# The order of four engines handed to a list scheduler inside the kernel, in a packed-attention plus feed-forward kernel

## The chip, the core and the metric

The kernel runs on one core of a Trainium2 chip. The core has a matrix engine (TensorE, PE in the profile, with its weight loads shown apart as PEld), a vector engine (VectorE, DVE), a scalar engine (ScalarE, ACT), a general engine (GpSimd, POOL) and a sync engine (SyncE, SP) that here only issues transfers. Each engine works through its own list of instructions in the order in which the program put them, and semaphores make one wait for another. Matmuls write to PSUM, which has 8 banks of 128 partitions by 512 fp32 numbers; ACT and DVE move the results on to SBUF. DMA queues carry data between HBM and SBUF.

The metric is the device time of one execution in microseconds (us).

## The reference: what is computed

For 8 batch entries and 8 heads, 32 learned "packs" `p` attend over 576 keys, and then the 576 queries attend over the 32 packed values. The result, as 4608 rows of 512, goes through a gated feed-forward layer.

```python
def _attn_ref(q, k, v, p):            # q, k, v: (8, 8, 576, 64); p: (8, 8, 32, 64)
    def sm_attn(qq, kk, vv):
        s = scale * np.matmul(qq, kk.transpose(0, 1, 3, 2))
        s = s - np.max(s, axis=-1, keepdims=True)
        a = np.exp(s)
        a = a / (np.sum(a, axis=-1, keepdims=True) + 1e-09)
        return np.matmul(a, vv)
    p_packed = sm_attn(p, k, v)
    return sm_attn(q, p_packed, p_packed)

def _moe_ref(x, w_in, w_out):         # x: (4608, 512); w_in: (512, 2048); w_out: (2048, 512)
    h = x @ w_in
    sp = np.maximum(h, 0.0) + np.log1p(np.exp(-np.abs(h)))
    g = h * erf(sp)
    return (g @ w_out).astype(np.float32)
```

`w_in` and `w_out` arrive as 64-bit floats and are turned into 32-bit ones by bit operations on the chip.

## The kernel before, in words

All 8 heads of a batch entry `b` lie side by side on the partitions. `attention(b)` (`first_attention` for `b` = 0) makes the first scores `s1` in two halves of 288 columns, their softmax `a1`, its transposes `t1` and, with `v`, the packed values `pt` (product `p`; the last 64 of the 576 keys go through a small transpose of their own, the left-over, line 368). Then it makes the second scores `s2`, again in two halves, and their softmax, which is kept as a high and a low part, `a2h` and `a2l`.

Since the second attention is linear in `pt`, the kernel multiplies `pt` into `w_in` first: `w_prime(b, j)` makes piece `j` of four of a matrix W' (tile `wp`, kept as `wph` and `wpl`). The feed-forward then runs in 128 units: one per batch entry and 128 columns `f` of the 2048. A unit's `h` is two halves (`h_part`), each of six matmuls into one of the two `ps_h` banks, evacuated by an ACT copy to `hs` (line 469). Units are gated in groups (`gate_group`, mostly of four): all Softplus, then all Erf (each needs its table of functions loaded into ACT), then on DVE a product and a split into `gh` and `gl`. Finally `o_part` adds the unit to four accumulators of 128 rows (`ps_o0` to `ps_o3`), in three matmuls each. The last 64 rows of two batch entries are collected through a DRAM buffer `rest` and done together by `o_rest` (tile `or`, 48 matmuls a pair, loaded in four tiles `g`).

PSUM is full: four banks for `o`, two for `h`, and two (`ps_m`, one tile over both) shared by scores, transposes, `p`, W' and the last `or`.

**What sets the order before.** The program text puts attention stages, weight pieces and W' pieces behind chosen units by the tables of `PLAN`. The framework's own scheduler may then move instructions on each engine; functions on ACT are held in their order (`in_turn`), conversions are held behind a named copy (`hold`), and from unit 48 on (`"strict": 48`) PE keeps exactly the text's order (`pe`). Each half of the scores and each W' piece takes the one `ps_m` tile, one at a time. Four staging buffers for 64-bit weights are borrowed from the W' pool (`EARLY`), in the order in which `do` comes to the pieces of `w_in` and `w_out`; after those, two `wst` buffers serve all weight pieces and also the `g` tiles of `or`.

Lines that the steps below touch: 87 (weight loads), 97 to 102 (their conversion), 166 to 176 (first loads), 325 and 388 (`s1`, `s2`), 350 and 399 (the two Exp), 369 (left-over copy), 374 (`p`), 391 (DVE transposes out of `s2`), 420 to 423 (W'), 443 and 446 (Softplus, Erf), 467 and 469 (`h` and its copy), 489 (`o`), 510 and 513 (`g`, `or`).

## Time and profile before

| | us |
|---|---|
| median of 3 runs (lowest, highest) | 787.98 (783.42, 790.71) |
| time of the profiled execution | 785.28 |
| its span, first to last instruction | 783.4 |
| PE busy | 732.7 (94%) |
| ACT busy | 496.8 (63%) |
| DVE busy | 436.6 (56%) |
| HBM traffic over the span | 54.00 MB read, 19.92 MB written |

The profile shows one execution. A row of a timeline gives start, length, engine, line, operation and, in brackets, how long the engine had been idle before it and who released it. Matmuls overlap: one lasts longer than the distance to the next, so their rate is read from the starts. The profile counts an fp32 matmul as two. PEclk is the clock that PE was granted, as a share of full speed.

### The profile page before, as it was taken

The page shows a single profiled execution, that of the slowest core. Times are in us where ns is not written, and L with a number is a line of the kernel's source. Part 1 is how long each engine was busy: PE and PEld are TensorE (multiplying, and loading weights), DVE is VectorE, ACT ScalarE, POOL GpSimd, SP SyncE. Part 2 cuts the span into 40 slices and gives each one's busy share as a digit, 9 for nine tenths or more (in the row PEclk, how much of TensorE's full clock was granted, in tenths as well). Part 3 has the DMA queues.
Part 4 walks back from the last instruction along what each step waited for, and adds up shares of the span by engine and source line. Part 5 has one row for each costly group of instructions (what it writes and reads, how often), then busy time and mean ns, then how long its engine had stood idle before and what let it go on. Part 6 is the DMA issues. An engine that isn't in the chain of part 4 may idle for free.

```text
span 783.4 us, 12901 instructions
## 1 busy us (share of the span) xinstructions
PE 732.7 (94%) x5008; PEld 581.9 (74%) x5008; DVE 436.6 (56%) x689; ACT 496.8 (63%) x806; POOL 8.0 (1%) x14
## 2 busy tenths in 40 slices
PE   4576899989999999999999999999999999999997
PEld 3273678668777877878777787778877887788885
DVE  3778967678764247544755048553674236743530
ACT  3284988788668556685767348675676457666731
POOL 0000000000101000000000000000000000000000
PEclk9986999999999999999999999999999999999999
DMA  9915153443716230223302332124212320003103
GB/s 334 337 36 192 45 170 98 163 125 99 205 33 147 60 127 13 66 68 114 96 16 65 126 90 68 24 68 153 68 43 61 118 67 13 16 14 98 41 21 121
DMA packets 66397, 74.77 MB, mean 95 GB/s; under 512 B 40224, under 2 KB 42272, under 8 KB 66336
## 3 DMA queue, kind: packets, MB, share of 16 engines
q1 hardware_dynamic: 64896, 71.27, 29.2%
q0 software_dynamic: 1152, 2.10, 1.8%
q8 instruction: 39, 0.64, 0.3%
q10 hardware_dynamic: 288, 0.59, 0.2%
q14 instruction: 22, 0.18, 0.1%
HBM read 54.00 MB, written 19.92 MB: 94 GB/s over the span
## 4 chain that ended last, share of the span: by engine, by line
PE 73%; ACT 12%; DVE 10%; DMA 3%; issue 2%; SPq 0%; DVEq 0%; ACTq 0%
PE o L489 38%; PE h L467 22%; PE or L513 5%; PE wp L420 3%; ACT t L446 2%; PE p L374 2%; ACT L446 2%; DVE hs L448 2%; ACT t L443 2%; ACT hs L469 1%; DMA g<-rest 1%; ACT L443 1%; PE s L325 1%; DVE ta L397 1%; DVE mx L396 1%
## 5 line engine op out<-in xcount | busy, mean ns | idle before, releaser
L489 PE MATMUL o<-woh,gh 128*128 128x512 f32 x512 | 201.8, 405 | 1.3 <-DVE gh L432 1.0
L489 PE MATMUL o<-woh,gl 128*128 128x512 f32 x512 | 201.8, 394 | 0.9 <-DVE gl L433 0.9
L469 ACT COPY hs<-h 128x288 f32<-128x288 f32 x256 | 98.2, 396 | 164.3 <-PE h L467 162.9
L489 PE MATMUL o<-wol,gh 128*128 128x512 f32 x512 | 200.7, 395 | 0.0
L467 PE MATMUL h<-a2h,wph 128*128 128x288 f32 x512 | 158.6, 310 | 18.0 <-ACT hs L469 10.4
L448 DVE TENSOR_TENSOR hs<-t,hs 128x576 f32<-128x576 f32 x128 | 91.8, 753 | 115.0 <-ACT t L446 115.0
L467 PE MATMUL h<-a2h,wpl 128*128 128x288 f32 x512 | 154.2, 302 | 1.0 <-DVE wpl L423 1.0
L467 PE MATMUL h<-a2l,wph 128*128 128x288 f32 x512 | 154.6, 302 | 0.0
L467 PEld LDWEIGHTS h<-a2h,wph 128*128 128x128 f32 x512 | 99.7, 195 | 47.0 <-ACT hs L469 16.2
L489 PEld LDWEIGHTS o<-woh,gh 128*128 128x128 f32 x512 | 96.6, 189 | 41.2 <-issue 23.8
L489 PEld LDWEIGHTS o<-wol,gh 128*128 128x128 f32 x512 | 96.3, 188 | 23.0 <-issue 2.1
L432 DVE CAST gh<-hs 128x576 fp32r<-128x576 f32 x128 | 58.2, 456 | 94.0 <-PE o L489 94.0
L489 PEld LDWEIGHTS o<-woh,gl 128*128 128x128 f32 x512 | 96.6, 189 | 16.6 <-issue 1.7
L467 PEld LDWEIGHTS h<-a2l,wph 128*128 128x128 f32 x512 | 99.9, 195 | 10.0 <-DVE mx L252 0.9
L467 PEld LDWEIGHTS h<-a2h,wpl 128*128 128x128 f32 x512 | 99.8, 195 | 2.4 <-DVE wpl L423 1.3
L433 DVE TENSOR_TENSOR gl<-hs,gh 128x576 fp32r<-128x576 f32 x128 | 96.2, 754 | 2.3
L443 ACT ACTIVATE t<-hs 128x576 f32<-128x576 f32 x128 | 87.4, 685 | 2.7
L446 ACT ACTIVATE t<-t 128x576 f32<-128x576 f32 x128 | 78.1, 674 | 0.4
L420 PE MATMUL wp<-w_in_sb,pt 64*32 64x512 f32 x512 | 44.3, 646 | 6.3 <-ACT a L301 3.4
L423 DVE TENSOR_TENSOR wpl<-wp,wph 128x1024 fp32r<-128x1024 f32 x32 | 39.0, 1220 | 16.7 <-ACT wph L422 16.0
L443 ACT ACT_TABLE_LOAD x37 | 47.5, 1283 | 0.7
L446 ACT ACT_TABLE_LOAD x37 | 47.5, 1283 | 0.7
(112 smaller groups left out, 565.6 us busy)
## 6 DMA issues: line engine op xcount, KB each, us to landing
q<-qT SPq DMA_DIRECT2D x32, 288.0 KB, 4.5
v<-v SPq DMA_DIRECT2D x32, 256.0 KB, 4.2
wos<-w_out SPq DMA_DIRECT2D x16, 512.0 KB, 3.7
out<-ob SPq DMA_DIRECT2D x32, 256.0 KB, 2.3
g<-rest SPq DMA_DIRECT2D x16, 512.0 KB, 3.3
k<-kT SPq DMA_DIRECT2D x26, 288.0 KB, 4.0
wi<-w_in SPq DMA_DIRECT2D x12, 512.0 KB, 4.1
rest<-gh SPq DMA_DIRECT2D x128, 32.0 KB, 1.5
```

The source lines that it names most:

```text
L374: pe(nc.tensor.matmul(po[64 * r:64 * r + 64, NK * c:NK * c + NK], values[j][0:n, 64 * (2 * c + r):64 * (2 * c + r) + 64], a1t[0:n, j, r, N ...
L420: pe(nc.tensor.matmul(ps[NK * c:NK * c + NK, r, :], pt[b][64 * r:64 * r + 64, NK * c:NK * c + NK], w_in_sb[64 * r:64 * r + 64, c, j * FB:( ...
L423: nc.vector.tensor_tensor(lo[:], ps[:], hi[:], op=ALU.subtract)
L432: nc.vector.tensor_copy(ghi[:], hs[:])
L433: nc.vector.tensor_tensor(glo[:], hs[:], ghi[:], op=ALU.subtract)
L443: in_turn(nc.scalar.activation(t[:], hs[:], AF.Softplus))
L446: in_turn(nc.scalar.activation(t[:], t[:], AF.Erf))
L448: nc.vector.tensor_tensor(hs[:], t[:], hs[:], op=ALU.mult)
L467: pe(nc.tensor.matmul(ps[:, 0:HT], w[:, r, fo:fo + P], a[:, r, c, :], start=(m == 0), stop=(m == 5)))
L469: hold.append(nc.scalar.copy(hs[:, c * HT:(c + 1) * HT], ps[:, 0:HT]).ins.name)
L489: pe(nc.tensor.matmul(acc[b][x][:], gg[:, x * P:(x + 1) * P], w[:], start=(first and n == 0), stop=(last and n == 2)))
L513: pe(nc.tensor.matmul(acc["rest"], gg, w[:], start=(k == 0 and i == 0 and n == 0), stop=(k == NFB - 1 and i == PER - 1 and n == 2)))
```

## The change

The program is first recorded and only then issued. Every instruction group becomes an `Op` with an engine, a key (the unit at which it is wanted), an estimated length and the buffers that it reads and writes. `Program.order()` plays these through: whenever an engine is free it takes the waiting `Op` with the lowest key whose buffers have room, counting 1.283 us for each change of ACT table and an extra for PE's change between tile shapes; an Exp is not taken inside a group of Softplus or Erf. The order found is then fixed on PE, ACT, DVE, SP and POOL by `line`, from the first instruction on. The tables of places in `PLAN` give way to keys.

Further edits:

- From `b` = 2 on, the second half of `s1` and of `s2` and the odd W' pieces (`j` = 1, 3) go to the two `ps_h` banks in place of `ps_m`, and are evacuated bank by bank (two smaller copies in place of one).
- The left-over of `a1`'s transposes has its own tile `a1r` (tag `rem`), and its eight matmuls of `p` are an `Op` of their own.
- The first two attentions reduce their scores straight from PSUM; the `k` of `b` = 0 is loaded in halves, and ACT's first table load stands ahead of ACT's loads.
- The four borrowed staging buffers all go to the four pieces of the second quarter of `w_in`.
- The first units' groups end after 2, 5, 8, 12, 16 units (before: 2, 5, 7, 9, 12, 14, 16).
- `or` is sixteen `Op`s of three matmuls in place of four blocks of twelve.
- The instructions on PE are the same in number and shape. ACT has 90 table loads (before 88) and 23 instructions more in all, DVE 29 more.

```diff
-    "strict": 48,
+    "lag": 5.5,
+    "steady": (0, 1, 1.5, 2, 2, 5, 5.2, 6, 7, 8, 8, 9, 10, 11),
+    "merge": (1, 1),
...
+    def order(self):
...
+            for engine, line in ready.items():
+                if free[engine] > now + 1e-9:
+                    continue
+                held, pick = set(), None
+                for i, (_, _, op) in enumerate(line):
+                    if op.run == "exp" and state["within"]:
+                        continue
...
+                    if any(room[t] < n or t in held for t, n in need.items()):
+                        held.update(need)
+                        continue
+                    pick = i
+                    break
+                if pick is None:
+                    continue
+                op = line.pop(pick)[2]
+                op.fresh = [buf for buf in op.used if buf.tag and buf not in taken]
+                for buf in op.fresh:
+                    taken.add(buf)
+                    room[buf.tag] -= 1
+                op.start, busy = now, op.busy
+                if op.run:
+                    if op.run != state["table"]:
+                        busy += self.LOAD
+                        state["table"] = op.run
+                    state["within"] = op.kind == 1
+                if engine == "PE":
+                    if op.kind != state["kind"]:
+                        busy += self.SWITCH[state["kind"]]
+                    state["kind"] = op.kind
+                free[engine] = now + busy
...
+    def line(engine, ins):
+        names = {last[x] for x in (engine, *fresh) if x in last}
+        for name in names:
+            tc.add_manual_dep(ins.ins, name, mybir.DependencyInfo(
+                mybir.DependencyClass.NoSync, mybir.DependencyReason.DATA), reason="order")
+        for x in (engine, *fresh):
+            last[x] = ins.ins.name
+        fresh.clear()
+        return ins
...
+    staged = [0]
     EARLY = ("wpl", "wpl", "wph", "wph")
...
+        tag = EARLY[staged[0]] if staged[0] < len(EARLY) else "wst"
+        staged[0] += 1
+        st = buf(tag, [P, n], name, I64)
+        dma(sent, n * P * 8, lambda: nc.sync.dma_start(st[:], src), (st,), ())
...
-    pe_last, strict = [], [False]
-
-    def pe(ins):
-
-        if strict[0] and pe_last:
-            follow(ins, pe_last[-1])
-        pe_last[:] = [ins.ins.name]
...
+    def banks_of(names, where):
+        if where == "m":
+            one = buf("ps_m", [P, 2, 512], names)
+            return [lambda: one[:, 0, :], lambda: one[:, 1, :]], (one,), lambda: one[:]
+        tags = ("ps_h", "ps_h") if where == "h" else (f"ps_o{2 * where}", f"ps_o{2 * where + 1}")
+        two = [buf(t, [P, 512], f"{names}_{y}") for y, t in enumerate(tags)]
+        return [lambda: two[0][:], lambda: two[1][:]], tuple(two), None
...
+    def product(key, names, where, left, right, r, after=()):
+
+        banks, w, whole = banks_of(names, where)
+
+        def emit():
+            return [mm(banks[i]()[NK * c:NK * c + NK, 0:HT], left(i, c), right(i, c), start=True, stop=True)
+                    for c in range(NC) for i in range(2)]
+        return banks, w, whole, pe(key, S_US, emit, w, r, 1, after)
...
+            where = (("m", 0), (0, 1))[b][x] if roomy else ("m", "h" if PLAN["merge"][0] else "m")[x]
...
+        ar = buf("rem", [P, 2 * P], f"a1r{b}")
...
+            where = x if first else ("m", "h" if PLAN["merge"][0] else "m")[x]
...
+    def w_prime(key, b, j, where="m"):
+        hi, lo = (buf(t, [P, 2, FB], f"{t}{b}_{j}", F32R) for t in ("wph", "wpl"))
+        banks, w, whole = banks_of(f"wp{b}_{j}", where)
...
+        if whole:
+            act(key, 1024, lambda: nc.scalar.copy(hi[:], whole()), (hi,), w)
+            dve(key, 1024, lambda: nc.vector.tensor_tensor(lo[:], whole(), hi[:], op=ALU.subtract), (lo,), w + (hi,))
...
+                act(key, 512, lambda r=r: nc.scalar.copy(hi[:, r, :], banks[r]()), ((hi, r),), (w[r],))
+                dve(key, 512, lambda r=r: nc.vector.tensor_tensor(lo[:, r, :], banks[r](), hi[:, r, :], op=ALU.subtract),
+                    ((lo, r),), (w[r], (hi, r)))
...
-            for n, (gg, w) in enumerate(terms((g[:, 0, i], g[:, 1, i]), k * PER + i)):
-                pe(nc.tensor.matmul(acc["rest"], gg, w[:],
-                                 start=(k == 0 and i == 0 and n == 0),
-                                 stop=(k == NFB - 1 and i == PER - 1 and n == 2)))
-        if k < NFB - 1:
-            return
-        ob = tpool.tile([P, DM], F32, name=f"obr{pair}", tag="ob")
-        nc.scalar.copy(ob[:], acc["rest"])
...
+
+    def o_rest(key, pair):
+
+        final = pair == B // 2 - 1
+        to = buf("ps_m", [P, 2, 512], f"or{pair}") if final else buf("ps_o0", [P, 512], f"or{pair}")
+        for k in range(NFB):
+            g = buf("wst", [P, 2, PER, 2 * REM], f"g{pair}_{k}", F32R)
+            dma(key - 1, P * 8 * 2 * REM * 4, lambda g=g, k=k: nc.sync.dma_start(
+                g[:].bitcast(F32), rest[pair, k].rearrange("p x i two t -> p x i (two t)")), (g,), (), after=sent_rest[pair, k])
+            for i in range(PER):
+                whi, wlo = wo_hi[k * PER + i], wo_lo[k * PER + i]
+                pe(key, 0.693, lambda k=k, i=i, g=g, whi=whi, wlo=wlo: [
+                    mm(to[:, 0, :] if final else to[:], gg, w[:], start=(k == 0 and i == 0 and m == 0),
+                       stop=(k == NFB - 1 and i == PER - 1 and m == 2))
+                    for m, (gg, w) in enumerate(((g[:, 0, i], whi), (g[:, 1, i], whi), (g[:, 0, i], wlo)))],
+                   (to,), (g, whi, wlo))
+        done(key, f"obr{pair}", to, 2 * pair * S + NT * P)
 
...
-        wait = PLAN["wait"]
-        sent_at = max(sent_at + 1, close[m] + wait[min(m // G, len(wait) - 1)])
-        here = parts.setdefault(min(sent_at, N + m), [])
-        here += [(o_part, (b, f, first, last, x)) for x in (1, 2, 3, 0)]
-        if b % 2 and f == NF - 1:
-            here += [(o_rest, (b // 2, k)) for k in range(NFB)]
-    for n in range(N + NF):
-        strict[0] = n >= PLAN["strict"]
-        here = parts.get(n, [])
-        some = (len(here) + 1) // 2
-        if n < N:
-            h_part(n, 0)
-        for block, what in here[:some]:
-            block(*what)
-        if n < N:
-            h_part(n, 1)
-            do(plan.pop(n, []))
-        for block, what in here[some:]:
-            block(*what)
...
+            w_prime(piece_use[b, j] - PLAN["wp"], b, j, "m" if j % 2 == 0 or b < NB0 or not PLAN["merge"][1] else "h")
+            made += 1
...
+    for n, (b, f, first, end) in enumerate(units):
+        prepare(n)
+        h_unit(n, b, f)
+        close = n + 1 in ends
+        if close:
+            for m in range(n + 1):
+                if (units[m][0], units[m][1]) in gs:
+                    o_unit(m, *units[m])
+                    if units[m][0] % 2 and units[m][1] == NF - 1:
+                        o_rest(m + PLAN["lag"] + PLAN["rest"], units[m][0] // 2)
+
+    for op in prog.order():
+        fresh.update(x.tag for x in op.fresh)
+        op.emit()
```

Three places of the new order, word for word. First SP, the loads behind the first attention's: names `wi1_c` are the four pieces of the second quarter of `w_in`, `wos` pieces of `w_out`, `p2` and `k_2` inputs of `b` = 2. Before:

```order
L87 DMA wi1_2_470<-w_in 128x512
L87 DMA wos2_477<-w_out 128x512
L307 DMA p2_1130<-pT 128x128
L281 DMA k0_2_1132<-kT 128x576
L281 DMA k1_2_1134<-kT 128x576
L87 DMA wos0_384<-w_out 128x512
L87 DMA wos1_432<-w_out 128x512
L87 DMA wi1_0_371<-w_in 128x512
L87 DMA wi1_1_377<-w_in 128x512
```

Now:

```order
L293 DMA wi1_0_245<-w_in 128x512
L293 DMA wi1_1_256<-w_in 128x512
L293 DMA wi1_2_266<-w_in 128x512
L293 DMA wi1_3_269<-w_in 128x512
L293 DMA wos0_271<-w_out 128x512
L293 DMA wos1_273<-w_out 128x512
L352 DMA p2_288<-pT 128x128
```

The piece `wi1_3`, which before is issued seven rows further down, behind four writes to `rest`, now goes out in the first run of loads.

Second ACT, between the third unit of `b` = 4 and the fifth: `hs` are the copies out of `h`, `t` the Softplus (L443, now L541) and Erf (L446, now L546), `a1_5` the Exp of the next attention (L350, now L433). Before:

```order
L443 ACTIVATE t4_3_4113<-hs4_3_4084 128x576
L446 ACT_TABLE_LOAD
L446 ACTIVATE t4_0_4107<-t4_0_4107 128x576
L446 ACTIVATE t4_1_4109<-t4_1_4109 128x576
L446 ACTIVATE t4_2_4111<-t4_2_4111 128x576
L446 ACTIVATE t4_3_4113<-t4_3_4113 128x576
L350 ACT_TABLE_LOAD
L350 ACTIVATE a1_5_4026,sm5_4028<-a1_5_4026,m5_4027 128x576 x2
L469 COPY hs4_4_4153<-h4_4_0_4154 128x288
L469 COPY hs4_4_4153<-h4_4_1_4168 128x288
```

Now:

```order
L541 ACTIVATE t4_3_4178<-hs4_3_4162 128x576
L433 ACT_TABLE_LOAD
L433 ACTIVATE a1_5_3958,sm5_4183<-a1_5_3958,m5_4116 128x576
L546 ACT_TABLE_LOAD
L546 ACTIVATE t4_0_4032<-t4_0_4032 128x576
L576 COPY hs4_4_4221<-h4_4_0_4185 128x288
L576 COPY hs4_4_4221<-h4_4_1_4200 128x288
L546 ACTIVATE t4_1_4085<-t4_1_4085 128x576
```

Ahead of the two copies stand now one Exp and one Erf with their table loads, where before stood four Erf and two Exp with theirs; the second Exp moved behind a later group of Softplus.

Third PE, the second scores of `b` = 5 (`s2`). Before, the first half and the row behind it, the first of many of `o` and `h`:

```order
L388 MATMUL s2_0_5_4517<-q0_5_4018,pt5_4456 32x288 x2
L388 MATMUL s2_0_5_4517<-q1_5_4020,pt5_4456 32x288 x2
L388 MATMUL s2_0_5_4517<-q2_5_4022,pt5_4456 32x288 x2
L388 MATMUL s2_0_5_4517<-q3_5_4024,pt5_4456 32x288 x2
L489 MATMUL o4_0_3_4357<-woh2_483,gh4_2_4134 128x512
```

Now:

```order
L270 MATMUL s2_5_0_4557<-q0_5_4120,pt5_4519 32x288 x2
L270 MATMUL s2_5_0_4557<-q1_5_4500,pt5_4519 32x288 x2
L270 MATMUL s2_5_0_4557<-q2_5_4502,pt5_4519 32x288 x2
L270 MATMUL s2_5_0_4557<-q3_5_4514,pt5_4519 32x288 x2
L270 MATMUL s2_5_1_0_4568<-q0_5_4120,pt5_4519 32x288
L270 MATMUL s2_5_1_1_4570<-q0_5_4120,pt5_4519 32x288
L270 MATMUL s2_5_1_0_4568<-q1_5_4500,pt5_4519 32x288
```

The second half (`s2_5_1_0` and `s2_5_1_1`, the two `ps_h` banks) now follows the first at once; before, it came two units later. The two halves of `s1` of `b` = 4 to 7 and the W' pieces are not neighbours in the new order: between them stand `o` and `h` rows.

More of the change, by code (lines that the diff above doesn't have):

```diff
@@ L1 @@
 from contextlib import ExitStack
+import bisect
+import heapq
 import concourse.bass as bass
@@ L27 @@
-    "wait": (5, 3, 4, 4, 2),
-    "strict": 48,
-    "first": 4,
-    "hold": 1,
-}
-F64_SCALE = 2.0 ** -112
+    "lag": 5.5,
+    "act": 2.6,
+    "dve": 1.4,
+    "copy": 2.0,
+    "steady": (0, 1, 1.5, 2, 2, 5, 5.2, 6, 7, 8, 8, 9, 10, 11),
+    "second": (-12, -12, -12, -6, -6, -5, -4, -2, -1, 1, 1, 2, 3, 4),
+    "third": (8, 10, 11, 14, 14, 17, 18, 20, 21, 24, 24, 25, 26, 27),
+    "wp": 3.0,
+    "wi": 5.0,
+    "wo": 3.0,
+    "conv": 1.0,
+    "rest": 0.5,
+    "ends": (2, 5, 8, 12, 16),
@@ new lines, with __init__, __getitem__, t @@
+    "merge": (1, 1),
+}
+class Buf:
+    def __init__(self, tag, name, make):
+        self.tag, self.name, self.make, self.tile, self.parts, self.users = tag, name, make, None, {}, []
+    def __getitem__(self, index):
+        return self.t[index]
+    @property
+    def t(self):
+        if self.tile is None:
+            self.tile = self.make()
+        return self.tile
+class Op:
+    def __init__(self, engine, key, busy, dur, emit, run):
+        self.engine, self.key, self.busy, self.dur, self.emit, self.run = engine, key, busy, dur, emit, run
+        self.deps, self.fresh, self.used, self.start, self.kind = set(), [], [], None, 0
@@ new lines, in pe, with act, dve @@
+    def pe(key, busy, emit, w, r, kind=0, after=()):
+        return prog.add("PE", key, busy, 0.2, lambda: [line("PE", i) for i in emit()], w, r, kind=kind, after=after)
+    def act(key, n, emit, w, r, run=None, kind=0, more=0.0, after=()):
+        return prog.add("ACT", key, act_us(n) + more, 0.15, lambda: line("ACT", emit()), w, r, run=run, kind=kind, after=after)
+    def dve(key, n, emit, w, r, twice=False, after=()):
+        return prog.add("DVE", key, dve_us(n, twice), 0.14, lambda: line("DVE", emit()), w, r, after=after)
@@ new lines, in attention @@
+            if first and j == NCH - 1:
+                load_w_in_pair(keys[1], WIK[0][0], 0)
+                load_w_in_pair(keys[1], WIK[0][1], 2)
+        q = load("q", qT, "kvq" if b else "t0", keys[2])
+        big = lambda name, shape: buf("big", shape, f"{name}{b}")
+        a = big("a1_", [P, 2, S])
+        m, sm = buf("m", [P, 2], f"m{b}"), buf("sm", [P, 2], f"sm{b}")
+        ms = buf("ms", [P, 2, 2], f"ms{b}") if roomy else None
+        if first:
+            act(-99, 0, lambda: nc.scalar.preload_act_table_set("exp_and_others"), (), (), run="exp", kind=0)
@@ new lines, in attention, with gather @@
+        act(keys[7], 2 * P, lambda: nc.scalar.copy(ar[0:REM, :], pr()[0:REM, 0:2 * P]), (ar,), ((w[0], "r"),))
+        def gather(js):
+            return [mm(po()[64 * r:64 * r + 64, NK * c:NK * c + NK],
+                       values[j][0:min(P, S - j * P), 64 * (2 * c + r):64 * (2 * c + r) + 64],
+                       at[:, j, r, NK * c:NK * c + NK] if j < NT else ar[0:REM, r * P + NK * c:r * P + NK * c + NK],
+                       start=(j == 0 and c == 0), stop=(j == NCH - 1), skip_group_check=True)
+                    for j in js for c in range(NC) for r in range(2)]
@@ new lines, in done @@
+    def done(key, name, to, at, which=None):
+        ob = buf("ob", [P, DM], name)
+        act(key - 1, DM, lambda: nc.scalar.copy(ob[:], to[:] if which else to[:, 0, :] if to.tag == "ps_m" else to[:]),
+            (ob,), (to,))
+        if which is None:
+            for x in range(2):
+                t0 = at + x * S
+                dma(key, REM * DM * 4, lambda x=x, t0=t0: nc.sync.dma_start(out[t0:t0 + REM, :], ob[x * REM:(x + 1) * REM, :]),
+                    (), (ob,))
+        elif which in begun:
+            dma(key, P * DM * 4, lambda: nc.gpsimd.dma_start(out[at:at + P, :], ob[:], accum_op=ALU.add), (), (ob,), "POOL")
+        else:
+            dma(key, P * DM * 4, lambda: nc.sync.dma_start(out[at:at + P, :], ob[:]), (), (ob,))
+        begun.add(which)
```

820 lines of the change are left out of this document (377 added, 443 removed).

## The prediction

> **What bounds the kernel now.** I read the page first, then the windows (busy us of each engine in a stretch, with the granted clock), then the waits.
>
> ```profile
> span 783.4 us, 12901 instructions
> PE 732.7 (94%) x5008; PEld 581.9 (74%) x5008; DVE 436.6 (56%) x689; ACT 496.8 (63%) x806; POOL 8.0 (1%) x14
> PEclk9986999999999999999999999999999999999999
> ```
>
> PE is the bound, 94% busy. The change leaves its instructions as they are, so it can only act on PE's idle 783.4 - 732.7 = 50.7 us, on the half clock near the start (the 8 and the 6 in PEclk), and on what PE pays between tile shapes.
>
> ```profile
> 0.00:40.00 40.00, 20.85 (x216) 12.47 (x217) 23.34 (x42) 11.56 (x22) 0.69 (x6) 1.00 0.92 330
> 40.00:80.00 40.00, 29.69 (x238) 21.84 (x236) 31.59 (x58) 27.49 (x46) 0.00 (x0) 0.74 0.33 111
> 80.00:120.00 40.00, 36.90 (x208) 29.02 (x209) 32.48 (x53) 35.19 (x55) 0.00 (x0) 1.00 0.35 106
> 240.00:280.00 40.00, 40.00 (x309) 31.52 (x308) 15.35 (x27) 27.41 (x46) 3.54 (x4) 1.00 0.52 131
> ```
>
> The columns are PE, PEld, DVE, ACT, POOL, clock, DMA share, GB/s. The idle time lies at the start: 19.2 us before 40 us, 10.3 us in the next 40 (at 0.74 of the clock), 3.1 us up to 120; by 240 there is none to be seen. The waits say who is late:
>
> ```profile
> ACT hs L469 <- PE h L467: 162.9, 123, 3.9
> PE p L374 <- ACT a1t L369: 2.6, 5, 0.5
> PE or L513 <- DMA g<-rest: 2.0, 3, 0.9
> ```
>
> ACT waits 162.9 us for PE, PE little for anyone; what is left are small waits at fixed places.
>
> **The rates.** Two pieces of the chain with nothing else in them:
>
> ```profile
> 119.12 1.59 PE h L467 x12
> 746.10 20.44 PE o L489 x90
> ```
>
> An `h` matmul takes 1.59 / 12 = 0.1325 us, an `o` matmul 20.44 / 90 = 0.227.
>
> **Term A, the start.** The landmarks of before, on PE unless said:
>
> ```profile
> 41.85 0.79 ACT L350 ACTIVATE a<-a,m 128x576 f32<-128x576 f32 x1
> 45.83 0.61 PE L467 MATMUL h<-a2h,wph 128*128 128x288 f32 x1 [3.63 <-ACT hs L469]
> 46.23 0.44 PE L467 MATMUL h<-a2l,wph 128*128 128x288 f32 x1
> 46.47 0.44 PE L467 MATMUL h<-a2h,wpl 128*128 128x288 f32 x1
> 56.42 2.64 PE L374 MATMUL p<-a1t,v 128*64 128x32 f32 x80 [0.46 <-ACT a1t L369]
> 60.16 0.33 SPq L87 DMA_DIRECT2D wi<-w_in  x1
> 63.95 0.74 ACT L97 ACTIVATE w_in_sb<-wi 128x512 f32<-128x512 f32 x1 [2.62 <-DMA wi<-w_in]
> 61.96 0.72 PE L388 MATMUL s<-q,pt 64*32 64x288 f32 x16
> 67.39 2.40 PE L420 MATMUL wp<-w_in_sb,pt 64*32 64x512 f32 x16 [2.89 <-DVE ta L391]
> 70.90 0.61 PE L467 MATMUL h<-a2h,wph 128*128 128x288 f32 x1 [1.11 <-ACT wph L422]
> ```
>
> The second W' piece of `b` = 0 starts at 67.39, and unit 4 only at 70.90. Two things hold it: its last piece of `w_in` is issued at 60.16 and converted from 63.95, and it shares `ps_m` with the attention of `b` = 1, which runs from its Exp (41.85) over `p` (56.42) and `s2` (61.96). The new order issues that piece in the first run of loads, so the attention alone is left. Its `s1` now stands ahead of the first `h`, and its maxima are taken from PSUM between the steps of `b` = 0's softmax:
>
> ```profile
> 36.56 0.76 DVE L258 TENSOR_TENSOR a2l<-tb,a2h 128x576 fp32r<-128x576 f32 x1 [0.74 <-ACT a2h L255]
> ```
>
> These steps end at 37.3 now, so I put the Exp at 38, 4 us earlier. From Exp to `p` before takes 14.6 us, with the wait of 3.63 us; in the new order stand four half units at the half clock (6 x 0.24 us each, from the starts 46.23 and 46.47: 5.8 us), two Exp and the transposes with their copy, an estimate of 9.5: lead 9. From `p` to `s2` before takes 5.5 us; now `p` (2.64) and one half unit (1.45): lead 10. From `s2` to W' before takes 5.4 us, 2.89 of it a wait for DVE; the second half now has banks of its own, so two products of 0.72 and four transposes (0.46 each, row below) make about 3: lead 12.5, W' at 55. But before had by then done the 24 `o` matmuls of units 0 and 1, 24 x 0.227 = 5.4 us, which the new order puts behind: 7 us are left. Three waits right behind unit 4 go as well, since their W' and gates come earlier:
>
> ```profile
> 73.19 0.61 PE L467 MATMUL h<-a2h,wpl 128*128 128x288 f32 x1 [0.97 <-DVE wpl L423]
> 80.90 1.18 PE L489 MATMUL o<-woh,gh 128*128 128x512 f32 x4 [1.00 <-DVE gh L432]
> 84.45 0.40 PE L467 MATMUL h<-a2h,wph 128*128 128x288 f32 x1 [1.02 <-ACT hs L469]
> ```
>
> Together 3.0. What works against it: on ACT a conversion of `w_in` now stands ahead of the first copies of transposes and waits for its load (a second or so), and the first half of `b` = 0's softmax waits for the second half's scores. I put no more than the rounding up of my steps against these: A = -10, between -3 (all of it eaten) and -13 (the whole lead).
>
> [...] The row: after 3.63 us idle, `h` matmuls start 0.24 us apart in place of 0.1325. [...]
>
> **Term B, the wait near 160.**
>
> ```profile
> 160.09 1.25 PE L420 MATMUL wp<-w_in_sb,pt 64*32 64x512 f32 x16 [3.44 <-ACT a L301]
> ```
>
> W' waits 3.44 us for ACT to empty `ps_m` of the second half of `s1`. That half now lies in the `h` banks and nothing of W' waits for it. What is late next is the first half's `ps_m`, which follows a W' piece: 0.7 left. B = -2.7, between 0 and -3.4.
>
> **Term C, the steady waits.** Each batch entry from `b` = 3 on has the same ones; first and last of four, one of four, and the two rows of the waits view above:
>
> ```profile
> 339.22 0.40 PE L467 MATMUL h<-a2h,wph 128*128 128x288 f32 x1 [1.18 <-ACT hs L469]
> 606.03 0.40 PE L467 MATMUL h<-a2h,wph 128*128 128x288 f32 x1 [1.18 <-ACT hs L469]
> 386.34 0.40 PE L467 MATMUL h<-a2h,wph 128*128 128x288 f32 x1 [0.18 <-ACT hs L469]
> ```
>
> The 1.18 comes from the place on ACT shown above: four Erf and two Exp with their loads ahead of two `h` copies. Now one Exp and one Erf stand there, some 2.9 us less, and the wait goes: 4 x 1.18 = 4.7. The 0.18: 4 x 0.18 = 0.7. `p` waited four times 0.5 for the left-over's copy (2.6 in all, less the 0.46 of the start: 2.1); with a tile of its own the other 32 matmuls go first. `g`: 2.0 us in all, of which 0.9 at the very end stays, since the last `or` still has nothing behind it; 1.1 goes, because twelve `or` matmuls now take some 6 us with `h` and `o` between. C = -8.6, between 0 and that.
>
> **Term D, changes of tile shape.** A half of `s2` alone, and its price:
>
> ```profile
> 460.39 0.29 PE L467 MATMUL h<-a2h,wpl 128*128 128x288 f32 x1
> 460.62 0.72 PE L388 MATMUL s<-q,pt 64*32 64x288 f32 x16
> 461.26 0.50 PE L489 MATMUL o<-woh,gh 128*128 128x512 f32 x1
> 461.60 0.40 PE L489 MATMUL o<-woh,gl 128*128 128x512 f32 x1
> 23.04 2.17 PE L238 MATMUL s<-q,pt 64*32 64x288 f32 x32 [2.73 <-DVE pt L225]
> 24.96 1.96 PE L420 MATMUL wp<-w_in_sb,pt 64*32 64x512 f32 x16
> ```
>
> The `h` is over at 460.52, and the `o` behind `s` needs 0.34 us instead of 0.227: the half costs 0.85. A pair at the half clock takes 24.96 - 23.04 = 1.92, so 0.96 a half, or 0.48 at the full clock: a neighbour saves up to 0.37. The order has such pairs six times in `s2` (-2.2 at most), hardly in `s1` and not in W'; and it cuts `p` in two seven times (+2.5 at most by the same price). D = 0, between -2 and +2.
>
> **Term E, new waits in the `h` banks.** From `b` = 2 on four pieces a batch entry (24 in all) take both `h` banks, so `h` stands still until they are emptied. The nearest rows for emptying them are copies of that size and the transposes:
>
> ```profile
> L127 ACT CAST woh<-wo 128x512 fp32r<-128x512 f32 x16 | 9.9, 620 | 7.0 <-DVE wo L102 7.0
> L128 DVE TENSOR_TENSOR wol<-wo,woh 128x512 fp32r<-128x512 f32 x16 | 11.0, 685 | 7.8 <-ACT woh L127 7.8
> L391 DVE STREAM_TRANSPOSE ta<-s 128x288 f32<-128x288 f32 x28 | 11.9, 461 | 27.2 <-PE s L388 27.2
> L443 ACT ACT_TABLE_LOAD x37 | 47.5, 1283 | 0.7
> ```
>
> Behind a W' piece the first bank is free after 0.62 + 0.685 = 1.3 us and nine `o` matmuls (2.0 us) cover it; behind `s2` three or four transposes (up to 1.84) stand against six `o` (1.36). So 0.5 for each of six `s2` and 0.06 for the eighteen others: E = +4. Below, 0; above, see the rivals.
>
> **Beside other work.** ACT's 23 and DVE's 29 further instructions and two table loads (2 x 1.283) lie in ACT's 162.9 us of waiting: nothing; with that cover gone, about 12 us. SP's loads now keep a fixed order behind the writes to `rest`, and a late DVE would hold those behind it; the traffic after 40 us (share 0.33) leaves room.
>
> The sum: -10 - 2.7 - 8.6 + 0 + 4 = -17.3. The profiled execution took 785.28 (its span and 1.9 around it), so 768.0; the median of the runs, 787.98, lies 2.7 above that execution. Forecast 768.
>
> **The rivals.**
> - ACT eats the start's gain. For: ACT is busy 35.19 of 40 us from 80 on, and the new order has the same conversions to do in less time. Against: between 40 and 80 it has 12.5 us free. A shrinks to -3: 775.
> - The half clock lasts to unit 8. Units 4 to 7 of `h`, some 33 `o` and two W' are 48 x 0.1325 + 33 x 0.227 + 2 = 16 us; at half the clock 16 more, half of it under ACT's work: +8, 776. [...]
> - More goes than I counted: all of PE's idle time after 40 us but the tail's 5, 50.7 - 19.2 - 5 = 26.5, and the half clock of 40 to 80, 0.26 x 29.69 = 7.7. That is 34: 751.
> - Slower: the 24 pieces in the `h` banks each wait on an ACT that is at a table load. For: ACT and DVE keep their order, so a late copy holds PE behind both banks. Price 1.283 and what follows it, 1.4 each: 24 x 1.4 = 34 against the other terms' 21.3, so 785.28 - 21.3 + 34 = 798. It decides from 24 waits of 0.9 (no gain), and of 1.2 for slower by 1%. Against: six to nine `o` stand behind each piece.
> - It does not do what it says: W' pieces are not neighbours, and if the new order elsewhere only changes places of waits, C and E cancel and A is small: 783.
>
> **How the numbers follow.** Forecast 0.47 (758 to 774); ACT 0.17; clock 0.08; more 0.12; slower 0.10; cancelled 0.06. About 1% (8 us) can be told from no change. Faster by more than that: 0.47 + 0.12 and two thirds of the two at 775 and 776, 0.76; within: the rest of these and the cancelled, 0.13; slower 0.11. The range runs from 752 to 784: it leaves out the slower case and the end of "more".
>
> **What would show it.** Right: W' of `b` = 0 (second piece) before 58 us; the clock at 1.00 from 60 on; no row of 3.44 near 160; no wait of 1.18 for `hs` and none of 0.5 ahead of `p`; `g` waits only at the end; waits of up to 0.5 on DVE's transposes behind `s2`. Wrong: PE waiting over 1 us for the ACT or DVE instructions that empty the `h` banks; ACT without a gap up to 120 us and PE idle there; a half clock after 60.

## The result, and the profile after

The changed kernel took **753.61 us** (median of 4 runs, 751.96 to 755.44), the kernel before 788.6 beside it. The ratio is **0.957, with a 95% interval of 0.951 to 0.962**: 4.3% faster, 35 us. A second measurement, with more runs, gave 0.959 (0.956 to 0.962). The forecast was 768, its range 752 to 784; the sum of terms came to -17.3 us, and between the two profiled executions (785.28 and 754.75) 30.5 us are gained, 1.8 times that. Of the rivals, "more goes than I counted" (751, chance 0.12) is the one that happened in size, though not in its make-up: it reckoned with 26.5 us of PE's idle time, of which 14.0 went.

From the page of the changed kernel's profiled execution (span, PE, granted clock in 40 slices):

```profile
span 753.0 us, 12964 instructions
PE 716.3 (95%) x5008; PEld 573.3 (76%) x5008; DVE 433.9 (58%) x718; ACT 497.9 (66%) x829; POOL 8.4 (1%) x14
PEclk9898999999999999999999999999999999999999
```

PE has the same 5008 instructions as before, but is busy for 16.4 us less, and idle for 36.7 us instead of 50.7: of the 30.4 us by which the span is shorter, 14.0 are idle time and 16.4 are matmuls that ran closer together. The windows (PE, PEld, DVE, ACT, POOL, clock, DMA share, GB/s):

```profile
0.00:40.00 40.00, 20.55 (x220) 13.44 (x220) 24.69 (x51) 14.27 (x30) 0.70 (x6) 0.91 0.92 319
40.00:80.00 40.00, 34.13 (x302) 25.94 (x301) 35.71 (x63) 34.89 (x57) 0.00 (x0) 0.91 0.32 100
80.00:120.00 40.00, 38.18 (x229) 30.18 (x229) 31.70 (x57) 30.58 (x55) 0.00 (x0) 0.98 0.56 172
240.00:280.00 40.00, 39.69 (x318) 31.88 (x319) 16.43 (x27) 20.99 (x33) 0.00 (x0) 1.00 0.32 94
```

The clock column can't be compared up to 40 us, since a stretch without a clock record counts as full: in the kernel before the records begin at 41.4 us, and its 1.00 stands beside a pair of score halves that takes 2.17 us at 23.04, where a pair at full clock takes 1.20 (at 349.02, under term D).

The stretch from 40 to 80 us changed most: 34.13 us of PE at 0.91 of the clock, where before there were 29.69 at 0.74. ACT is fuller there (34.89 instead of 27.49), and it still waits for PE 168.6 us in all, while PE hardly waits for its copies any more:

```profile
ACT hs L576 <- PE h L270: 168.6, 134, 4.7
PE h L270 <- ACT hs L576: 1.5, 3, 0.6
```

The places that the prediction named, on PE (all matmuls but the transposes now stand on line 270):

```profile
35.56 0.85 PE L270 MATMUL h<-a2h,wph 128*128 128x288 f32 x2 [8.10 <-ACT a2h L511]
54.41 1.09 PE L270 MATMUL wp<-w_in_sb,pt 64*32 64x512 f32 x16 [1.15 <-DVE ta L488]
57.06 0.61 PE L270 MATMUL h<-a2h,wph 128*128 128x288 f32 x1 [1.55 <-ACT wph L525]
116.60 1.05 PE L270 MATMUL wp<-w_in_sb,pt 64*32 64x512 f32 x4 [1.82 <-DVE w_in_sb L279]
252.97 0.41 PE L458 MATMUL p<-ident,a 128*64 128x128 f32 x2 [0.31 <-ACT a1t L452]
346.57 0.37 PE L270 MATMUL h<-a2h,wph 128*128 128x288 f32 x1 [0.68 <-DVE wpl L530]
742.61 0.73 PE L270 MATMUL or<-woh,g 128*128 128x512 f32 x2 [0.70 <-DMA g<-rest]
```

The second W' piece of `b` = 0 starts at 54.41 (before 67.39, forecast 55). There is a new wait of 1.82 at 116.60, where a piece of `w_in` comes late. The 1.18 for `hs`, the 3.44 near 160 and the 0.5 ahead of `p` are gone; in the steady part (from 240 us on) there are left 0.31 ahead of the left-over's transpose three times, 0.68 behind a W' piece in the `h` banks twice, and 0.70 for `g` at the end.

**Where the time came from.** For each stretch I took its length less what its matmuls need at the rates of undisturbed stretches (`h` 0.1325 us, `o` and `or` 0.2275, a score half 0.72, a W' piece 1.0, a transpose 0.11, a `p` matmul 0.0335; counts and starts from the timelines). What is left is lost to idle time, half clock and changes of shape. Single entries are good to about 1 us.

| lost, us | 0 to 40 | 40 to 120 | 120 to 240 | 240 to the end | sum |
|---|---|---|---|---|---|
| before | 29.0 | 25.9 | 11.3 | 31.7 | 97.9 |
| changed | 29.2 | 14.9 | 4.9 | 18.7 | 67.7 |
| early loads alone (b1, below) | 28.8 | 32.3 | 12.8 | 31.7 | 105.6 |
| Exp later alone (b2) | 29.1 | 26.9 | 10.2 | 35.6 | 101.8 |
| one copy first alone (b3) | 28.8 | 29.3 | 15.8 | 32.2 | 106.1 |
| changed, without its two changes of shape (c1) | 28.6 | 15.1 | 4.8 | 13.6 | 62.1 |
| changed, ACT's copies free (e9) | 31.6 | 28.0 | 20.1 | 68.0 | 147.7 |

So 10.8 us came from the start, 6.4 from 120 to 240, and 13.0 from the steady part.

### The profile page after: what moved, and what is told of

Its sections match the earlier page's. It is cut to its first block, busy times and chain, and to the rows that moved or that the text cites. A ratio compares the mean times of both kernels' runs of the same rounds, so it can differ in the third digit from the quotient of the medians.

```text
span 753.0 us, 12964 instructions
## 1 busy us (share of the span) xinstructions
PE 716.3 (95%) x5008; PEld 573.3 (76%) x5008; DVE 433.9 (58%) x718; ACT 497.9 (66%) x829; POOL 8.4 (1%) x14
## 4 chain that ended last, share of the span: by engine, by line
PE 78%; ACT 10%; DMA 6%; DVE 4%; SPq 1%; issue 1%; DVEq 0%; ACTq 0%
PE o L270 43%; PE h L270 24%; PE or L270 4%; PE wp L270 4%; DMA wi<-w_in 2%; PE s L270 2%; ACT t L546 2%; PE p L270 2%; ACT L546 1%; DMA q<-qT 1%; ACT t L541 1%; DVE hs L551 1%; ACT hs L576 1%; ACT L433 1%; ACT L541 1%
## 5 line engine op out<-in xcount | busy, mean ns | idle before, releaser
L576 ACT COPY hs<-h 128x288 f32<-128x288 f32 x256 | 99.9, 400 | 168.6 <-PE h L270 168.6
L270 PE MATMUL o<-woh,gh 128*128 128x512 f32 x512 | 207.4, 405 | 0.0
L270 PE MATMUL h<-a2h,wph 128*128 128x288 f32 x512 | 155.0, 303 | 13.3 <-ACT a2h L511 8.1
L270 PE MATMUL h<-a2l,wph 128*128 128x288 f32 x512 | 152.1, 298 | 0.0
L270 PE MATMUL h<-a2h,wpl 128*128 128x288 f32 x512 | 151.7, 297 | 0.4 <-DVE wpl L526 0.4
L551 DVE TENSOR_TENSOR hs<-t,hs 128x576 f32<-128x576 f32 x128 | 94.6, 752 | 55.9 <-ACT t L546 55.5
L270 PEld LDWEIGHTS h<-a2h,wph 128*128 128x128 f32 x512 | 97.3, 190 | 32.6 <-ACT a2h L511 8.6
L270 PEld LDWEIGHTS h<-a2l,wph 128*128 128x128 f32 x512 | 97.4, 191 | 7.9 <-DVE a2l L512 0.3
L270 PEld LDWEIGHTS h<-a2h,wpl 128*128 128x128 f32 x512 | 97.3, 190 | 0.8 <-DVE wpl L526 0.8
L541 ACT ACTIVATE t<-hs 128x576 f32<-128x576 f32 x128 | 87.3, 686 | 2.5
L546 ACT ACTIVATE t<-t 128x576 f32<-128x576 f32 x128 | 83.7, 688 | 0.4
L546 ACT ACT_TABLE_LOAD x35 | 44.9, 1283 | 0.6
L541 ACT ACT_TABLE_LOAD x35 | 44.9, 1283 | 0.6
L270 PE MATMUL or<-woh,g 128*128 128x512 f32 x128 | 40.5, 398 | 0.7 <-DMA g<-rest 0.7
```

The lines of the kernel that those rows point to most:

```text
L270: return nc.tensor.matmul(*args, **kw)
L541: done.append(act(n + PLAN["lag"] - PLAN["act"] - 2, S, lambda t=t, hs=hs: nc.scalar.activation(t[:], hs[:], AF.Softplus), (t,), (hs,), ru ...
L546: erfs.append(act(e + PLAN["lag"] - PLAN["act"] - 4 + i, S, lambda t=t: nc.scalar.activation(t[:], t[:], AF.Erf), (t,), (), run="erf", kin ...
L551: dve(key, S, lambda t=t, hs=hs: nc.vector.tensor_tensor(hs[:], t[:], hs[:], op=ALU.mult), (hs,), (t,))
L576: act(n + c / 2 - PLAN["copy"], HT, lambda c=c, ps=ps: nc.scalar.copy(hs[:, c * HT:(c + 1) * HT], ps[:, 0:HT]), ((hs, c),), (ps,))
```

## The experiments

The theory was the prediction's: named waits go, each has its price, and the sum of them is the gain. The main rival grew out of the first four runs: the gain belongs to the order of all engines as one thing, and no named part carries it. Three runs do one part alone in the kernel before; the others undo one part in the changed kernel, whose scheduler then orders the engines anew.

### b1: the early loads alone

```diff
-    "wi": {1: (0, 0, 2, 3), 2: (7, 7, 10, 13), 3: (12, 14, 16, 16)},
+    "wi": {1: (0, 0, 0, 0), 2: (7, 7, 10, 13), 3: (12, 14, 16, 16)},
```

> The kernel before with one thing of the change alone: the four pieces of w_in that the second W' piece needs are loaded and converted first, ahead of the w_out pieces. My theory (the attention of b = 1 is what W' waits for, the row that ends its wait names DVE's transposes): the second W' piece of b = 0 moves by less than 2 us from 67.39, and the time by 0 to -2 us. Rival (the late load holds it): W' moves to about 62 and the time by -4 to -6 us.

Measured: 791.68 us against 786.51, ratio 1.008 (1.005 to 1.010): 5 us slower. On PE:

```profile
56.63 1.09 PE L420 MATMUL wp<-w_in_sb,pt 64*32 64x512 f32 x16 [0.27 <-ACT a1t L301]
64.28 2.64 PE L374 MATMUL p<-a1t,v 128*64 128x32 f32 x80
89.07 1.65 PE L420 MATMUL wp<-w_in_sb,pt 64*32 64x512 f32 x16 [4.81 <-DVE wpl L423]
95.46 2.04 PE L489 MATMUL o<-woh,gh 128*128 128x512 f32 x4 [4.74 <-DVE gh L432]
```

The W' piece came 10.8 us earlier (56.63, not 67.39), so the late load did hold it. Neither side of the expectation came true: W' moved further than the rival's 62, and the time rose. And W' did not come earlier on the old path: it now stands ahead of `p` of `b` = 1 (64.28, before 56.42) and of that entry's second scores (71.70, before 61.96), and no longer waits for their transposes. In the kernel before, load and attention end within 0.6 us of each other (transposes at 67.24, the last conversion at 67.81). The lead was worth nothing: 7.6 us less were lost up to 80 us, and 13.7 more from 80 to 120. There PE waits for `wpl` and the gates behind conversions and four table loads on ACT, and the half clock moved along, from 65.3 to 79.0 us before to 89.5 to 103.2.

### b2: the Exp later on ACT, alone

```diff
-    "steady": (1, 1, 1, 1, 2, 6, 6, 6, 7, 9, 11, 12, 13, 13),
+    "steady": (1, 1, 1, 1, 2, 5, 5, 7, 8, 9, 11, 12, 13, 13),
...
                 in_turn(one)        # one: the Exp of the first softmax
+                if b > 2:
+                    follow(one, hold[-1])
```

> The kernel before, with the two Exp of the first softmax of b = 3 to 7 placed on ACT behind the copies of hs of the fifth unit of the batch entry's run instead of directly behind four Erf; transposes, p and the steps up to s2 one unit later at most. My theory (term C): the four waits of 1.18 us for hs go, each worth up to 1.45 with the slower matmuls around it: 4.7 to 5.8 us less. Rival (the wait moves to the next copy or to the transposes): less than 1 us.

Measured: 793.38, ratio 1.011 (1.007 to 1.014): 7 us slower. The four waits of 1.18 are gone, and others stand in their place:

```profile
354.63 2.64 PE L377 MATMUL p<-a1t,v 128*64 128x32 f32 x80 [1.01 <-ACT a1t L372]
432.87 1.00 PE L516 MATMUL or<-woh,g 128*128 128x512 f32 x2 [2.48 <-ACT ob L497]
```

`p` waits 1.01 instead of 0.53, and `or` waits 2.48 for the copy of an accumulator, twice. What stood behind the Exp has got ahead, and what now stands behind them is waited for. All engines keep the order of the kernel before until 247 us and stand there within 0.3 us of its times, so the loss lies behind the edit.

### b3: one copy ahead of the Erf group, alone

```diff
             erf = nc.scalar.activation(t[:], t[:], AF.Erf)
             in_turn(erf)
+            if (2, 1) in a_copy:        # copy of the second half of s1 out of ps_m, b = 2
+                follow(erf, a_copy.pop((2, 1)))
```

(and the score step of `b` = 2 one unit earlier in the table, so that the copy stands ahead in the text)

> The kernel before, with one copy on ACT (second half of s1 of b = 2 out of ps_m) placed ahead of the Erf group instead of behind three of its Erf. Idle time alone: 3.4 us less. With the half clock that follows the wait (six h at 0.24 and four o at 0.40 instead of 0.1325 and 0.227): 5.1 us less. Rival (ACT has the same work, so the wait comes back at the next copies): under 1 us less.

Measured: 792.67, ratio 1.009 (1.005 to 1.012): 6 us slower.

```profile
160.81 1.09 PE L421 MATMUL wp<-w_in_sb,pt 64*32 64x512 f32 x16 [0.29 <-ACT a L301]
164.23 0.40 PE L471 MATMUL h<-a2h,wph 128*128 128x288 f32 x1 [2.33 <-ACT hs L473]
172.63 0.40 PE L471 MATMUL h<-a2h,wph 128*128 128x288 f32 x1 [3.82 <-ACT hs L473]
```

The 3.44 became 0.29, and 2.33 and 3.82 for `hs` came in its place. Not all of the loss is the edit's: ACT's order is that of the kernel before until 155.7 us, and there this trace is already 3.8 us late, with the clock at half from 84.6 to 91.4 us, where the kernel before ran at full. Of the 8.2 us between the two spans some 4.4 lie behind that place.

Each of the three edits removed the wait that it was aimed at, and each kernel was slower, by 5 to 7 us of the medians (for b3, part of that is not shown to be the edit's). I read these waits as places where ACT's backlog happens to show in the order of before; b2 and b3, with new waits behind ACT's copies, are the nearest to showing it.

### e1: nothing in the `h` banks

```diff
-    "merge": (1, 1),
+    "merge": (0, 0),
```

> The changed kernel with the second halves of s1 and s2 and all W' pieces back in ps_m, none in the h banks; its scheduler orders the engines anew. My term E as forecast (waits in the h banks cost 4 us): it is 0 to 4 us faster than the changed kernel. As its trace reads (no such waits, pairs of s2 save 0.35 us six times): 2 to 6 us slower. Rival (the h banks carry most of what was gained beyond the forecast): 10 us slower or more.

Measured: 752.53, ratio 0.957 (0.955 to 0.960): the same as the changed kernel. PE now waits at the start for `ps_m` and for `hs`, and from 164 us on for nothing but `g` at the end:

```profile
52.76 1.21 PE L270 MATMUL s<-q,pt 64*32 64x288 f32 x16 [2.97 <-DVE ta L488]
69.50 0.40 PE L270 MATMUL h<-a2h,wph 128*128 128x288 f32 x1 [2.15 <-ACT hs L576]
163.62 0.72 PE L270 MATMUL s<-q,pt 64*32 64x288 f32 x16 [1.75 <-DVE ta L488]
```

The pairing neither gained nor cost in the time; the 2 to 6 us slower that I had read from the trace did not come. In my count of lost time the steady part loses 14.8 us instead of 18.7, which is the size that term E had, and the first 240 us lose 49.3 instead of 49.0 (47.5 in the changed kernel's second profile). The rival, that the `h` banks carry the unexpected part, falls.

### e2: one piece of `w_in` late again

```diff
-            dve(ks[0], n, lambda wide=wide, blocks=blocks: nc.vector.tensor_tensor(blocks(), blocks(), wide(),
+            less = dve(ks[0], n, lambda wide=wide, blocks=blocks: nc.vector.tensor_tensor(blocks(), blocks(), wide(),
                                                                                    op=ALU.subtract), rd, mxp)
+            if b == 1:
+                marks.append(less)
...
-        dma(sent, n * P * 8, lambda: nc.sync.dma_start(st[:], src), (st,), ())
+        dma(sent, n * P * 8, lambda: nc.sync.dma_start(st[:], src), (st,), (), after=after)
...
-               w_in[c * P:(c + 1) * P, j * FB:(j + 1) * FB], f"wi{j}_{c}")
+               w_in[c * P:(c + 1) * P, j * FB:(j + 1) * FB], f"wi{j}_{c}", marks if (j, c) == (1, 3) else ())
```

> The changed kernel with the load of one piece of w_in held back until DVE is done with the second softmax's subtraction of b = 1 (it then goes out near 60 us as before); its scheduler orders the engines anew around that. Theory (in the new order the early piece is worth its lead): W' of b = 0, second piece, from 54.4 back to about 64, the time up by 5 to 9 us. Rival (as in the kernel before, where the early piece alone moved W' by 10.8 us and gained nothing): within 2 us.

Measured: 760.74, ratio 0.968 (0.965 to 0.970): 6.6 us slower than the changed kernel (754.13 in its own longest series, a2 below).

```profile
65.17 1.92 PE L270 MATMUL wp<-w_in_sb,pt 64*32 64x512 f32 x4 [2.24 <-DVE w_in_sb L279]
```

W' ends its wait at 65.17. In the new order the early piece is worth 6.6 us; in the old order (b1) it cost 5. It has a price only together with the order around it. (The two edits are no mirror images: e2 holds back one piece, b1 brought forward two, with their conversions.)

### e4: `or` in blocks of twelve

```diff
-            for i in range(PER):
-                whi, wlo = wo_hi[k * PER + i], wo_lo[k * PER + i]
-                pe(key, 0.693, lambda k=k, i=i, g=g, whi=whi, wlo=wlo: [
...
+            pe(key, 2.772, lambda k=k, g=g, w12=w12: [
...
+                for i in range(PER)
```

> The changed kernel with or in four steps of twelve matmuls a pair instead of sixteen of three. My term C (1.1 us of waits for g are hidden by the split): 1 to 2 us slower. Rival (the matmuls between hide nothing that the order could not hide otherwise): within 1 us, or faster.

Measured: 756.95, ratio 0.964 (0.960 to 0.967): 2.8 us slower than 754.13, a little over the 1 to 2 expected; the two were not measured side by side.

```profile
238.77 0.73 PE L270 MATMUL or<-woh,g 128*128 128x512 f32 x2 [1.84 <-DMA g<-rest]
```

One wait for `g` of 1.84 came back, and the 0.68 behind W' stands five times, not twice.

### e5: `p` in one step

```diff
-            pe(keys[8], V_US * 0.8, lambda: gather(range(NT)), ((w[0], "o"),), [at] + values[:NT])
-        pe(keys[8], V_US / 5, lambda: gather((NT,)), ((w[0], "o"),), (ar, values[NT]))
+            pe(keys[8], V_US, lambda: gather(range(NCH)), ((w[0], "o"),), [at, ar] + values)
```

(`b` = 0 keeps its steps)

> The changed kernel with p in one step of 80 matmuls that waits for the copy of the left-over. My terms C and D (a wait of 0.5 comes back about four times, a cut of 0.33 goes seven times): 0 to 1 us faster or slower. Rival (the own tile is worth its 2.1 us of waits): 2 us slower.

Measured: 749.22, ratio 0.954 (0.951 to 0.956): 4 to 5 us faster than the changed kernel, more than expected. The wait of 0.5 for the left-over's copy did not come back, since the scheduler put an `o` over it:

```profile
248.10 0.41 PE L458 MATMUL p<-ident,a 128*64 128x128 f32 x2 [0.30 <-ACT a1t L452]
248.59 0.50 PE L270 MATMUL o<-woh,gh 128*128 128x512 f32 x1
249.48 2.06 PE L270 MATMUL p<-a1t,v 128*64 128x32 f32 x64
```

But around `p` itself little changes: from the end of the `h` ahead of the left-over's transpose, `p` costs 3.70 us in the changed kernel (2.91 and 0.79 in its two pieces) and 3.85 in e5 (1.06 for the transpose and 2.79). In my count of the lost time 17.5 us are lost from 240 us on (the changed kernel's second profile: 18.6), and 44.9 up to there (47.5). So most of the difference lies in the first 240 us, where everything was ordered anew. Why that came out better is not settled.

### a2, c1: the changed kernel again, and without both changes of shape

c1 takes e1 and e5 together.

> The changed kernel as it is, as the measure for the two runs beside it on the same chip: 752 to 755 us, ratio 0.955 to 0.960.

> The changed kernel without its two changes of shape: nothing in the h banks and p in one step of 80; the scheduler orders the engines anew. If the two add up as they measured alone (-1 and -4): 747 to 750 us. If the scheduler's own forecast of its length ranks orders (it is 5 us longer than for the changed kernel): 757 to 760. In either case most of the gain over the kernel before stays, if it belongs to the order.

Measured on one chip: the changed kernel 754.13 (753.13 to 756.65; ratio 0.959, 0.956 to 0.962), without both 750.13 (749.21 to 750.43; ratio 0.953, 0.951 to 0.956). The PE rows of the pages, first the changed kernel, then c1:

```profile
PE 716.5 (95%) x5008; PEld 573.2 (76%) x5008; DVE 433.7 (58%) x718; ACT 497.5 (66%) x829; POOL 8.5 (1%) x14
```

```profile
PE 714.3 (96%) x5008; PEld 573.6 (77%) x5008; DVE 434.6 (58%) x706; ACT 495.0 (66%) x811; POOL 8.4 (1%) x14
```

The whole gain, and 4 us more, is there without the pairs in the `h` banks and without the two steps of `p` (the left-over keeps its tile of its own in e5 and c1, so that tile was not tested). The two do not add up as measured alone (e5 alone had all of it), and the scheduler's own forecast, 5 us longer for c1, ranked the two the wrong way round. c1 beats both kernels; e5 beside it can't be told from it.

### e8, e9, e10: the order fixed on fewer engines

In all three PE's order, the order of the functions on ACT and the shape of the work are those of the changed kernel, and the program text is the same; only the ties that hold an engine to it are left out. e9 frees ACT's copies and conversions, e10 frees DVE, and e8 frees both, SP and POOL. That is near the rules that the kernel before has from unit 48 on, where conversions are held behind a named copy besides.

```diff
-        names = {last[x] for x in (engine, *fresh) if x in last}
+        held = (engine,) if engine in ("PE", "run") else ()     # e8; e9: all but "ACT"; e10: all but "DVE"
+        names = {last[x] for x in held + tuple(fresh) if x in last}
...
-        lambda: line("ACT", emit()), w, r, run=run
+        lambda: line("run" if run else "ACT", emit()), w, r, run=run     # e8 and e9
```

> The changed kernel, in which only PE's order and the order of the functions on ACT are fixed (as in the kernel before from unit 48 on); the copies on ACT, all of DVE and SP may be moved by the framework's scheduler, which starts from the same order. Theory (the gain is in the order of ACT's copies and of DVE around PE's, fixed together): 10 us slower or more, with waits of PE for ACT's copies of over 1 us. Rival (PE's order and the pieces' shape carry the gain): within 3 us.

> The changed kernel with everything fixed but the copies and conversions on ACT, which the framework's scheduler may move between the functions. Theory (PE waits for copies that stand behind four functions): most of the loss of the run with the old rules, 40 us or more slower than the changed kernel. Rival (it takes both engines, or DVE alone): under 15 us slower.

> The changed kernel with everything fixed but DVE's order. Theory (ACT's copies are what PE waits for): under 15 us slower. Rival (gates and wpl on DVE stand behind conversions): 40 us or more slower.

Measured: e8 844.97 us (ratio 1.076, 1.073 to 1.079), e9 832.88 (1.058, 1.055 to 1.062), e10 794.81 (1.012, 1.008 to 1.015). Against the changed kernel that is 91, 79 and 41 us: ACT's copies are most of it, as expected, but DVE alone costs more than the 15 us allowed and reaches the rival's 40, so both engines matter. The waits of PE in e9 and in e10 (in us, times, longest):

```profile
PE h L271 <- ACT hs L577: 23.4, 23, 2.8
```

```profile
PE h L271 <- ACT hs L577: 16.2, 9, 2.7
```

In e9 PE waits 23 times for a copy of `hs`, 23.4 us in all, in e10 9 times and 16.2, in the changed kernel 3 times and 1.5. One such place, on ACT and then on PE, in e9:

```profile
314.51 2.40 ACT L547 ACTIVATE t<-t 128x576 f32<-128x576 f32 x4
316.82 0.68 ACT L577 COPY hs<-h 128x288 f32<-128x288 f32 x2
317.52 1.28 ACT L542 ACT_TABLE_LOAD   x1
318.81 0.69 ACT L542 ACTIVATE t<-hs 128x576 f32<-128x576 f32 x1
319.40 0.99 ACT L526 CAST wph<-wp 128x1024 fp32r<-128x1024 f32 x1
320.30 1.15 ACT L512 CAST a2h<-tb 128x1152 fp32r<-128x1152 f32 x1
321.35 0.70 ACT L577 COPY hs<-h 128x288 f32<-128x288 f32 x2
321.80 0.40 PE L271 MATMUL h<-a2h,wph 128*128 128x288 f32 x1 [2.01 <-ACT hs L577]
```

And the same place in the changed kernel:

```profile
281.09 1.85 ACT L546 ACTIVATE t<-t 128x576 f32<-128x576 f32 x3
282.82 1.01 ACT L525 CAST wph<-wp 128x1024 fp32r<-128x1024 f32 x1
283.71 0.42 ACT L576 COPY hs<-h 128x288 f32<-128x288 f32 x1
284.15 1.28 ACT L541 ACT_TABLE_LOAD   x1
285.45 0.69 ACT L541 ACTIVATE t<-hs 128x576 f32<-128x576 f32 x1
286.04 1.14 ACT L511 CAST a2h<-tb 128x1152 fp32r<-128x1152 f32 x1
287.08 0.69 ACT L576 COPY hs<-h 128x288 f32<-128x288 f32 x2
```

The functions come in the same order and the loads are as many. In the changed kernel the conversion of W' and a copy of `hs` stand ahead of the table load, and between the copies of `hs` lie 3.0 us; in e9 W' slipped behind the load next to `a2h`, and between them lie 3.85, with PE waiting 2.01. Beside the waits, e9 fell to half the clock again and again: its mean granted clock is 0.932 (the changed kernel's 0.989). Of the 80.0 us by which its span is longer, 45.7 are idle time of PE and 34.3 are slower matmuls.

## Why the prediction was right and where it was not

**Right: the bound and the side.** PE's instructions stayed, and all of the gain is idle time, half clock and gaps between matmuls. The measured time lies in the range, near its lower end, but below the 758 to 774 that the forecast itself had (0.47). The terms came to -17.3 and measured -30.2: 0.8 more in A, 3.7 in B, 8.4 in C, D and E together.

**Term A, -10, measured -10.8** (0 to 120 us). The size held, and so did the path, step by step: the Exp of `b` = 1 from 38.27 (forecast 38), `p` at 46.59 (47.4), the second scores at 50.68 (52), W' at 54.41 (55), released by DVE's transposes as forecast once the load was early. But the lead alone is not worth what I gave for it: in b1 W' had 10.8 us of it, and the time rose. That the four half units between that Exp and `p` run at the half clock was an estimate: the clock is 0.50 from 32.8 to 39.6 us, and 1.00 from there to 56.7 (windows view). That the clock is full from 60 us on failed: it is 0.50 from 56.7 to 63.5, and again from 118.2 to 121.6.

**Term B, -2.7, measured -6.4** (120 to 240 us). The step that failed is that I priced the 3.44 us of waiting and not the half clock behind it, though its rate stands in my own section on the start: six `h` at 0.24 and four `o` at 0.4 lose some 1.5 us, the change of shape among them. The rest is a smaller loss in the last weights and W' pieces, spread too thin to name.

**Term C, -8.6.** With D and E the forecast for the steady part was -4.6; measured are -13.0. From 240 us on PE's listed idle time fell from 9.6 to 3.0 us, 6.6: the waits of C went as priced, and waits of 2.3 for W' and the left-over are new. The matmuls beside each of the eight waits for `hs` were 0.27 us slower as well (0.17 ahead, 0.10 behind), which had no term: 2.2. One half clock of 3.4 us in the kernel before, behind `p` (last section), cost 1.6 and is gone. Together 10.4 of the 13.0.

**Term D, 0, between -2 and +2.** The price was right. A pair of `s2` halves between two `o`:

```profile
348.70 0.40 PE L270 MATMUL o<-wol,gh 128*128 128x512 f32 x1
349.02 1.20 PE L270 MATMUL s<-q,pt 64*32 64x288 f32 x32
350.15 0.50 PE L270 MATMUL o<-woh,gh 128*128 128x512 f32 x1
350.49 0.40 PE L270 MATMUL o<-woh,gl 128*128 128x512 f32 x1
```

From 348.93 (where that `o` is through) to 350.15 are 1.22, and 0.11 too much for the next `o`: 1.33 instead of two times 0.85, 0.37 saved. The cut of `p` gives about as much back: from the end of the `h` ahead, `p` cost 3.60 us in the kernel before with its wait of 0.53 and costs 3.70 now with one of 0.31, so that the wait that C took away from `p` gained nothing there.

**Term E, +4, between 2.3 and 4.** PE's rows show two waits of 0.68 behind W' pieces and one of 0.89 for the transposes of `b` = 2, 2.3 in all; without the pieces there (e1) the steady part lost 4 us less and the time was the same. Against the slower rival (798): of 24 places, three show.

**What the sum missed.** It prices each wait as if the rest stayed, and takes idle time for the whole price of a wait. The half clock behind waits (1.5 in B, 1.6 in C) and the slower matmuls beside them (2.2) had no term, and the rest has no name. Three runs (b1, b2, b3) show that taking away one such wait alone does not gain in the order of before, c1 that the `h` banks and the two steps of `p` carry nothing, and e9 that PE's order with ACT's copies left free is 79 us worse. In the new order the waits went and few came in their place; that it is by the order of all engines that they were worth their price is what these runs point to. It is not shown for the start: the edits that act there alone (scores reduced straight from PSUM, `k` in halves, the borrowed staging buffers, the first groups) were never taken out of the changed kernel, so that for the 10.8 us up to 120 they stand as a rival. From 240 us on they no longer act, and 13.0 us were gained. Nor do the runs show which of the scheduler's choices on ACT did it, nor how PE's old order would do with ACT's copies fixed by hand.

## What to carry to other kernels

A wait at a fixed place behind a busy engine can be a place where that engine's backlog shows; before pricing its removal, ask what will stand in that engine's queue instead, and test one removal alone. Where a second engine empties PSUM for the first, the order of its copies between its functions belongs to the first one's order: fixed together they gained 4 to 5% here; PE's same order with only ACT's functions fixed beside it lost 7.6%, since that order was planned around the copies. The list scheduler's own length ranked the one pair on record wrongly (5 us longer planned, 4 shorter measured); only the runs told.
